# Sliding-window attention: one set of weights for all heads, spread on chip instead of through DRAM

## The chip, the cores and the metric

The kernel runs on one core of a Trainium2 chip. The metric is the device time of one execution in microseconds (us), lower is better. A core has engines with a queue each that work side by side: PE (TensorE, matmuls; PEld is its weight loads), DVE (VectorE), ACT (ScalarE), POOL (GpSimd, used for constants only) and SP (SyncE, which here only issues transfers). PE writes to PSUM, eight banks of 128 partitions by 512 float32; all else is in SBUF, 128 partitions wide. Sixteen DMA engines move data between DRAM and SBUF.

## The reference

A transformer block over 2048 positions of width 512, in bfloat16: an attention with a dilated sliding window (32 heads of 16, each position sees itself and seven earlier ones, two apart), then an MLP with a ReLU gate of width 1376.

```python
def _A_ref(x, wqkv, wo):                       # H = 32, Dh = 16, W = 8, dil = 2
    q, k, v = ...                              # (x @ wqkv), as (3, B, H, S, Dh)
    idx = pos[:, None] - (arange(W) * dil)[None, :]        # masked where < 0
    logits = einsum("bhsd,bhswd->bhsw", q, kg) * Dh ** -0.5
    attn = softmax(where(mask, logits, -1e9))
    o = einsum("bhsw,bhswd->bhsd", attn, vg)
    return o.reshape(B, S, D) @ wo

h  = x + _A_ref(layernorm(x), wqkv, wo)
xn = layernorm(h)
h2 = h + (relu(xn @ W_gate) * (xn @ W_up)) @ W_down
```

## The kernel before

The positions are cut into four chunks of 512 (`CS`). Everything inside a chunk is kept transposed: features on partitions, positions along the row. For each chunk:

1. *Norm and transposes* (`layernorm`): per block of 128 positions DVE takes statistics (L301, L304), ACT makes 1/sqrt (L311, L315), DVE writes the normalised rows `xn` (L324), PE transposes them into PSUM tile `tp` (L330) and ACT evicts that into `xnT` (L333).
2. *QKV* (L362): 12 groups of four matmuls 128x128 by 128x512; ACT evicts each (L370). A row block of 128 features holds 8 whole heads of 16 dims, so there are four row blocks `t`, each with heads of its own.
3. *Scores*: for each row block DVE multiplies q by the eight shifted views of k in one instruction of 128x4096 (L397, tile `big`). PE adds over the 16 dims of a head with column-tiled matmuls of 32 output rows (L409, weights `sel`). Two row blocks make a pair `p`, whose scores fill one PSUM bank: 16 heads by 8 window places.
4. *Softmax* per pair: exponent on ACT (L416), denominator by a matmul with `bmat` (L422), its reciprocal as exp(-ln) on ACT (L425, L428), the product with it on DVE (L431).
5. *Spreading the weights*: the weights (`ex`, 128x512) go to a DRAM tile `scr` (L434), and for each row block 8 transfers (one a head, 128 KB each) read them back, each copied to the 16 partitions of its head (L455), into a tile `big`.
6. *Value sum*: DVE multiplies `big` by the eight shifted views of v (L462), PE adds the eight places with identity matmuls (L466), ACT evicts into `OT` (L470).
7. *Output projection* with `wo` (L486), residual on DVE (L491), norm and transposes as in 1 into `hnT`.
8. *MLP*: 11 blocks of 128 (the last 96) features, up and gate (L508), eviction and ReLU on ACT (L512, L515), product on DVE into `gT` (L518), down-projection (L534), residual on DVE (L538), store by SP (L541).

The order of the work is made by a planner at build time (`Plan.order`): each step has an engine, an assumed duration, its dependencies, the buffers that it takes, and a priority; the engine that can start first takes the step that can start first (of those within 0.02 us, the one of lowest priority number). The result is one fixed order per engine, which the chip follows whatever the true durations are. Priorities put chunk `tk`'s norm at 100·tk - 86, QKV at 100·tk + 10, attention at + 20, its MLP at + 160. Assumed durations are, for instance, 0.216 for a matmul of 512 columns, 0.52 for an ACT eviction, 2.2 for a 128x4096 product.

PSUM before is cut into fixed parts: 3 banks for `mm`, 2 for `od`, 1 for `tp`, 2 for `at`.

Of the kernel before, what the change touches and what calls it, by code (L numbers as in the profile page):

```python
# [8 lines left out]
P = 128  # L9
# [110 lines left out]
def kernel(  # L120
# [11 lines left out]
    nc = tc.nc  # L132
# [17 lines left out]
    HPT = P // DH  # L150
    NPR = NT // 2
# [6 lines left out]
    dr = ctx.enter_context(tc.tile_pool(name="dr", bufs=1, space=bass.MemoryType.DRAM))  # L158
# [30 lines left out]
    scr = [[dr.tile([P, CS], BF16, name=f"scr{c}_{p}") for p in range(NPR)] for c in range(NCK)]  # L189


    for j in range(BPC):
        nc.sync.dma_start(x_sm[:, j:j + 1, :], x_rows[:, j:j + 1, :])
    wq_r = A_wqkv.rearrange("(dt p) f -> p dt f", p=P)
    for c in range(3):
        nc.scalar.dma_start(wqkv_sb[:, :, c * D:(c + 1) * D], wq_r[:, :, c * D:(c + 1) * D])
    for tk in range(1, NCK):
        nc.sync.dma_start(x_sm[:, tk * BPC:(tk + 1) * BPC, :], x_rows[:, tk * BPC:(tk + 1) * BPC, :])
    nc.sync.dma_start(wo_sb[:], A_wo.rearrange("(dt p) f -> p dt f", p=P))
    nc.sync.dma_start(wu_sb[:], B_W_up.rearrange("(dt p) f -> p dt f", p=P))  # L200
    nc.sync.dma_start(wg_sb[:], B_W_gate.rearrange("(dt p) f -> p dt f", p=P))
    nc.sync.dma_start(
# [3 lines left out]


    make_identity(nc, identity[:])
    nc.gpsimd.memset(eps_t[:], EPS)
    nc.gpsimd.memset(sel[:], 0.0)  # L210
    nc.gpsimd.memset(kT[:, :, 0:PADL], 0.0)
    nc.gpsimd.memset(vT[:, :, 0:PADL], 0.0)

    nc.gpsimd.iota(ind_i[:], pattern=[[1, HPT]], base=0, channel_multiplier=0)
    nc.gpsimd.iota(bm_i[:], pattern=[[8, 2], [0, 2], [1, HPT], [0, 4]], base=0, channel_multiplier=0)
    nc.gpsimd.iota(mk_i[:], pattern=[[1, PADL]], base=0, channel_multiplier=0)
    nc.gpsimd.iota(ci[:], pattern=[[0, 4]], base=0, channel_multiplier=1)
    ca = sb.tile([P, 4], I32, name="ca")
    tmp = sb.tile([P, 4], I32, name="tmp")
    V = nc.vector  # L220

    def ts(o, i, s1, op0, s2=None, op1=None):
        if op1 is None:
            V.tensor_scalar(out=o, in0=i, scalar1=s1, scalar2=None, op0=op0)
        else:
            V.tensor_scalar(out=o, in0=i, scalar1=s1, scalar2=s2, op0=op0, op1=op1)

    ts(ca[:, 0:1], ci[:, 0:1], 4, ALU.arith_shift_right)
    ts(tmp[:, 0:1], ci[:, 0:1], 6, ALU.arith_shift_right, 3, ALU.arith_shift_left)
    ts(tmp[:, 1:2], ci[:, 0:1], 2, ALU.arith_shift_right, 7, ALU.bitwise_and)  # L230
    ts(tmp[:, 2:3], ci[:, 0:1], 5, ALU.arith_shift_right, 1, ALU.bitwise_and)
    ts(tmp[:, 3:4], ci[:, 0:1], 3, ALU.bitwise_and)
    V.tensor_copy(out=cf[:, 0:1], in_=ca[:, 0:1])
    tf = sb.tile([P, 4], F32, name="tf")
    V.tensor_copy(out=tf[:], in_=tmp[:])
    V.tensor_tensor(out=cf[:, 1:2], in0=tf[:, 0:1], in1=tf[:, 1:2], op=ALU.add)
    ts(cf[:, 2:3], tf[:, 2:3], 4.0 * DIL, ALU.mult)
    ts(cf[:, 3:4], tf[:, 3:4], 1.0 * DIL, ALU.mult)
    V.tensor_tensor(out=cf[:, 2:3], in0=cf[:, 2:3], in1=cf[:, 3:4], op=ALU.add)
    V.tensor_copy(out=ind_f[:], in_=ind_i[:])  # L240
    V.tensor_copy(out=bm_f[:], in_=bm_i[:])
    V.tensor_copy(out=mk_f[:], in_=mk_i[:])
    ts(ind[:], ind_f[:], cf[:, 0:1], ALU.is_equal)
    ts(bmat[:], bm_f[:], cf[:, 1:2], ALU.is_equal)
    ts(mask[:], mk_f[:], cf[:, 2:3], ALU.is_ge)
    for w in range(4):
        V.tensor_copy(out=sel[:, w, :, w], in_=ind[:])


    xnT_s = slots(2, [P, NT, CS], BF16, "xnT")  # L250
    hnT_s = slots(2, [P, NT, CS], BF16, "hnT")
    qT_s = slots(2, [P, NT, CS], BF16, "qT")
    OT_s = slots(2, [P, NT, CS], BF16, "OT")
    big_s = slots(5, [P, W, CS], BF16, "big")
    gT_s = slots(17, [P, CS], BF16, "gT")
    ex_s = slots(2, [P, CS], BF16, "ex")
# [3 lines left out]
    up_s = slots(3, [P, CS], BF16, "up_sb")  # L260
    gr_s = slots(2, [P, CS], BF16, "gr")
    o_s = slots(3, [P, D], BF16, "o_out")
    st_s = slots(4, [P, V.BN_STATS_DIM], F32, "st")
    mv_s = slots(4, [P, BPC, V.BN_AGGR_DIM], F32, "mv")
    rs_s = slots(4, [P, BPC], F32, "rs")
    mm_s = slots(3, [P, CS], F32, "mm_ps", ps)
    od_s = slots(2, [P, D], F32, "od_ps", ps)
    tp_s = slots(1, [P, NT, P], BF16, "tp_ps", ps)
    at_s = slots(2, [P, CS], F32, "at_ps", ps)

    plan = Plan()
    add = plan.add

# [9 lines left out]
    for tk in range(NCK):  # L283
        xload[tk] = add("LD", 0.0, None, lat=[5.0, 10.5, 12.0, 13.5][tk])
    wload = {"q": add("LD", 0.0, None, lat=7.0), "k": add("LD", 0.0, None, lat=8.0),
             "v": add("LD", 0.0, None, lat=9.0), "o": add("LD", 0.0, None, lat=15.0),
             "u": add("LD", 0.0, None, lat=19.0), "g": add("LD", 0.0, None, lat=23.0),
             "d": add("LD", 0.0, None, lat=27.0)}

    def layernorm(tk, src_dep, dst_slots, pr, groups):  # L290

        dst = Buf(dst_slots)
        mv, rs = Buf(mv_s), Buf(rs_s)
        evs = []
        for grp in groups:
# [21 lines left out]

            l = add("ACT", 0.25, f_ln, ag, pr, take=[rs], use=[mv], lat=AL)
            e = add("ACT", 0.17, f_ex, [l], pr, use=[rs], lat=AL)
            for j in grp:  # L320
                xn, tp = Buf(xn_s), Buf(tp_s)

                def f_xn(j=j, xn=xn):
                    V.tensor_scalar(out=xn.t[:], in0=x_sm[:, tk * BPC + j, :],  # L324
                                    scalar1=mv.t[:, j, 0:1], scalar2=rs.t[:, j:j + 1],
                                    op0=ALU.subtract, op1=ALU.mult)

                def f_tp(xn=xn, tp=tp):
                    for t in range(NT):
                        nc.tensor.transpose(tp.t[:, t, :], xn.t[:, t * P:(t + 1) * P], identity[:])  # L330

                def f_ev(j=j, tp=tp):
                    nc.scalar.copy(out=dst.t[:, :, j * P:(j + 1) * P], in_=tp.t[:])  # L333
# [7 lines left out]
    for tk in range(NCK):  # L341
# [3 lines left out]
        groups = [[0, 1], [2, 3]] if tk == 0 else [[0, 1, 2, 3]]  # L345
        xnT, xev = layernorm(tk, [xload[tk]] * BPC, xnT_s, lnp, groups)
# [4 lines left out]
        if tk == 0:  # L351
            seq = [(c, t) for p in range(NPR) for t in (2 * p, 2 * p + 1) for c in (0, 1)]
            seq += [(2, t) for t in range(NT)]
        else:
            seq = [(c, t) for t in range(NT) for c in (0, 1)] + [(2, t) for t in range(NT)]
        for n, (c, t) in enumerate(seq):
# [3 lines left out]
            def f_mm(c=c, t=t, mm=mm, xnT=xnT):  # L360
                for dt in range(NT):
                    nc.tensor.matmul(mm.t[:], lhsT=wqkv_sb[:, dt, c * D + t * P: c * D + (t + 1) * P],  # L362
                                     rhs=xnT.t[:, dt, :], start=(dt == 0), stop=(dt == NT - 1))
# [18 lines left out]
        OT = Buf(OT_s)  # L382
        oev = {}
        for p in range(NPR):
            prods, pd = [], []
            apr = base + 20 + 6 * p
            for t in (2 * p, 2 * p + 1):
                pb = Buf(big_s)

                def f_pr(t=t, pb=pb, qT=qT, s0=s0):  # L390
                    kb = kT[:, t, PADL + s0: PADL + s0 + CS]
                    k8 = bass.AP(tensor=kb.tensor, offset=kb.offset,
                                 ap=[list(kb.ap[0]), [-DIL, W]] + [list(y) for y in kb.ap[1:]])
                    qb = qT.t[:, t, :]
                    q8 = bass.AP(tensor=qb.tensor, offset=qb.offset,
                                 ap=[list(qb.ap[0]), [0, W]] + [list(y) for y in qb.ap[1:]])
                    V.tensor_tensor(out=pb.t[:], in0=q8, in1=k8, op=ALU.mult)  # L397
# [20 lines left out]
            def f_mk(ex=ex):  # L418
                V.tensor_tensor(out=ex.t[:, 0:PADL], in0=ex.t[:, 0:PADL], in1=mask[:], op=ALU.mult)
# [167 lines left out]
```

## Time and profile before

| | us |
|---|---|
| median of 3 runs (lowest to highest) | 329.92 (328.26 to 330.45) |
| the profiled execution, whole | 326.86 |
| its span, first to last instruction | 325.1 |
| PE busy, in that span | 245.4 |
| DVE busy | 149.0 |
| ACT busy | 123.9 |
| mean clock granted to PE (1 is full) | 0.89 |

The profile is of one execution. A row of the groups of instructions reads: line, engine, operation, output<-inputs, shapes, xcount | busy us in all, mean ns of one | idle time of the engine just before them, and what ended it. A row of the waits reads: who waited <- for whom: us in total, times, longest. The chain that ended last is followed back from the last instruction, each step to what released it. DMA issues show the size of one transfer and the median us from issue to landing. Matmuls are pipelined: the length of a row of several is what counts, not the mean of one.

### The profile page before, as it was taken

To read this page: it belongs to the slowest core of one execution; us is meant where nothing else is said; L and a number is where in the kernel's file an instruction comes from. 1 tells how busy PE (TensorE), PEld (TensorE's weight loads), DVE (VectorE), ACT (ScalarE), POOL (GpSimd) and SP (SyncE) were. 2 spreads that over 40 slices of the span, in tenths; PEclk is the share of its full clock that TensorE was granted. 3 is DMA by queue.
4 is the path that set the end of the run, shared out by engine and by line. 5 is a ranking of instruction groups with operands and counts; after the bars stand their busy time and mean duration, and the time that the engine had idled before them with its cause. 6 is when DMAs were issued, how large, how long until landed. Compare 5 with 4: busy or idle time off the path is not lost.

```text
span 325.1 us, 3266 instructions
## 1 busy us (share of the span) xinstructions
PE 245.4 (75%) x1155; PEld 107.9 (33%) x1176; DVE 149.0 (46%) x235; ACT 123.9 (38%) x227; POOL 1.8 (1%) x14
## 2 busy tenths in 40 slices
PE   0597963489652695974999956999995556989995
PEld 0243421134210242531444422444442122444442
DVE  2989622487222589334131133748423323831222
ACT  2458632045300135732406612317872112226630
POOL 2000000000000000000000000000000000000000
PEclk9999897779856778995999987999998778999999
DMA  8991799939979101990010990010089990010001
GB/s 250 359 381 50 132 127 127 133 49 131 130 117 135 23 0 28 137 112 0 0 50 32 135 124 0 3 48 16 18 135 132 132 132 4 0 49 18 0 16 49
DMA packets 16352, 28.56 MB, mean 88 GB/s; under 512 B 2672, under 2 KB 11216, under 8 KB 16336
## 3 DMA queue, kind: packets, MB, share of 16 engines
q1 hardware_dynamic: 14752, 26.78, 48.6%
q10 hardware_dynamic: 1584, 1.57, 1.5%
q8 instruction: 9, 0.15, 0.2%
q14 instruction: 7, 0.06, 0.1%
HBM read 25.20 MB, written 3.15 MB: 87 GB/s over the span
## 4 chain that ended last, share of the span: by engine, by line
PE 40%; DMA 38%; DVE 8%; SPq 6%; ACT 4%; issue 4%; DVEq 0%; ACTq 0%
DMA big<-scr 33%; PE od_ps L534 12%; PE mm_ps L508 10%; PE mm_ps L362 8%; SPq L455 5%; PE od_ps L466 4%; DVE big L462 4%; DMA scr<-ex 3%; PE od_ps L486 2%; DMA x_sm<-in_A_x_dram 2%; PE at_ps L409 2%; PE tp_ps L330 1%; DVE st L301 1%; ACT xnT L333 1%; ACT rec L428 1%
## 5 line engine op out<-in xcount | busy, mean ns | idle before, releaser
L466 PE MATMUL od_ps<-big,identity 128*128 128x512 bf16 x124 | 45.4, 525 | 49.6 <-DVE big L462 38.5
L462 DVE TENSOR_TENSOR big<-big,vT 128x4096 bf16<-128x4096 bf16 x16 | 36.7, 2292 | 77.2 <-DMA big<-scr 71.8
L508 PE MATMUL mm_ps<-hnT,wu_sb 128*128 128x512 bf16 (+1 forms) x169 | 48.0, 404 | 8.4 <-ACT gr L515 6.4
L362 PE MATMUL mm_ps<-xnT,wqkv_sb 128*128 128x512 bf16 x187 | 47.2, 407 | 1.9 <-ACT xnT L333 1.4
L508 PE MATMUL mm_ps<-hnT,wg_sb 128*128 128x512 bf16 (+1 forms) x174 | 47.6, 395 | 0.4 <-DMA big<-scr 0.2
L466 PEld LDWEIGHTS <-identity 128*128 128x128 bf16 x128 | 14.8, 120 | 75.9 <-issue 37.6
L470 ACT CAST OT<-od_ps 128x512 bf16<-128x512 f32 x16 | 9.4, 585 | 80.4 <-PE od_ps L466 80.4
L534 PE MATMUL od_ps<-wd_sb,gT 128*128 128x512 bf16 (+1 forms) x173 | 39.2, 379 | 0.4 <-DVE x_sm L491 0.3
L518 DVE TENSOR_TENSOR gT<-gr,up_sb 128x512 bf16<-128x512 bf16 (+1 forms) x44 | 18.3, 422 | 45.6 <-ACT gr L515 45.4
L397 DVE TENSOR_TENSOR big<-qT,kT 128x4096 bf16<-128x4096 bf16 x16 | 35.7, 2284 | 4.9 <-ACT kT L370 4.9
L515 ACT ACTIVATE gr<-mm_ps 128x512 bf16<-128x512 f32 (+1 forms) x44 | 26.3, 597 | 29.1 <-PE mm_ps L508 16.3
L512 ACT CAST up_sb<-mm_ps 128x512 bf16<-128x512 f32 (+1 forms) x44 | 25.7, 584 | 14.7 <-PE mm_ps L508 12.3
L362 PEld LDWEIGHTS <-wqkv_sb 128*128 128x128 bf16 x192 | 20.1, 105 | 27.7 <-issue 9.4
L508 PEld LDWEIGHTS <-wu_sb 128*128 128x128 bf16 (+1 forms) x176 | 18.3, 105 | 30.8 <-issue 14.7
L508 PEld LDWEIGHTS <-wg_sb 128*128 128x128 bf16 (+1 forms) x176 | 18.4, 105 | 23.1 <-issue 4.7
L330 PE MATMUL tp_ps<-identity,xn 128*128 128x128 bf16 x128 | 13.6, 235 | 15.1 <-DVE xn L324 9.1
L534 PEld LDWEIGHTS <-gT 128*128 128x128 bf16 (+1 forms) x176 | 17.0, 98 | 20.3 <-issue 0.6
L301 DVE BATCH_NORM_STATS2 st<-x_sm 128x6 f32<-128x512 bf16 x32 | 20.8, 678 | 5.9 <-DMA x_sm<-in_A_x_dram 5.8
L538 DVE TENSOR_TENSOR o_out<-x_sm,od_ps 128x512 bf16<-128x512 bf16 x16 | 11.0, 687 | 24.1 <-PE od_ps L534 24.1
L330 PEld LDWEIGHTS <-xn 128*128 128x128 bf16 x128 | 10.2, 105 | 23.5 <-DVE xn L324 10.0
L486 PE MATMUL od_ps<-wo_sb,OT 128*128 128x512 bf16 x64 | 15.3, 379 | 0.0
L333 ACT COPY hnT<-tp_ps 128x512 bf16<-128x512 bf16 x16 | 9.3, 583 | 15.2 <-PE tp_ps L330 15.2
(49 smaller groups left out, 116.2 us busy)
## 6 DMA issues: line engine op xcount, KB each, us to landing
big<-scr SPq DMA_DIRECT2D x128, 128.0 KB, 7.9
out_dram<-o_out SPq DMA_DIRECT2D x16, 128.0 KB, 1.7
wqkv_sb<-in_A_wqkv_dram ACTq DMA_DIRECT2D x3, 512.0 KB, 5.9
x_sm<-in_A_x_dram SPq DMA_DIRECT2D x3, 512.0 KB, 8.3
wu_sb<-in_B_W_up_dram SPq DMA_DIRECT2D x1, 1376.0 KB, 10.9
wg_sb<-in_B_W_gate_dram SPq DMA_DIRECT2D x1, 1376.0 KB, 13.9
wd_sb<-in_B_W_down_dram SPq DMA_DIRECT2D x1, 1280.0 KB, 15.0
scr<-ex SPq DMA_DIRECT2D x8, 128.0 KB, 1.7
```

The lines of the kernel that those rows point to most:

```text
L301: V.bn_stats(out=st.t[:], in_=x_sm[:, tk * BPC + j, :])
L330: nc.tensor.transpose(tp.t[:, t, :], xn.t[:, t * P:(t + 1) * P], identity[:])
L362: nc.tensor.matmul(mm.t[:], lhsT=wqkv_sb[:, dt, c * D + t * P: c * D + (t + 1) * P], rhs=xnT.t[:, dt, :], start=(dt == 0), stop=(dt == NT ...
L397: V.tensor_tensor(out=pb.t[:], in0=q8, in1=k8, op=ALU.mult)
L462: V.tensor_tensor(out=ab.t[:], in0=ab.t[:], in1=v8, op=ALU.mult)
L466: nc.tensor.matmul(u.t[:], lhsT=identity[:], rhs=ab.t[:, w, :], start=(w == 0), stop=(w == W - 1))
L486: nc.tensor.matmul(od.t[:], lhsT=OT.t[:, t, j * P:(j + 1) * P], rhs=wo_sb[:, t, :], start=(t == 0), stop=(t == NT - 1))
L508: nc.tensor.matmul(mm.t[:fs, :], lhsT=w_sb[:, dt, ft * P: ft * P + fs], rhs=hnT.t[:, dt, :], start=(dt == 0), stop=(dt == NT - 1))
L512: nc.scalar.copy(out=ub.t[:fs, :], in_=um.t[:fs, :])
L515: nc.scalar.activation(out=gr.t[:fs, :], in_=gm.t[:fs, :], func=ACT.Relu)
L518: V.tensor_tensor(out=gt.t[:fs, :], in0=gr.t[:fs, :], in1=ub.t[:fs, :], op=ALU.mult)
L534: nc.tensor.matmul(od.t[:], lhsT=gts[ft].t[:fs, j * P:(j + 1) * P], rhs=wd_sb[:fs, ft, :], start=(ft == 0), stop=(ft == NFT - 1))
```

## The change

It re-cuts the features so that every row block holds dims of all heads. Columns `t, t+4, t+8, ...` of `wqkv` are taken as weights for block `t`, so a row block has 4 dims (`DQ`) of each of the 32 heads (partition = 4·head + dim), and the four blocks add to the same scores. `wo` is loaded with the matching row order. So there is one set of weights per chunk, in two halves `hf` of four window places: `ex` holds 4 places by 32 heads.

- Scores: a product of four places at a time (128x2048, tile `pb`), and per product four column-tiled matmuls with `sel` (128x32), accumulated over the four row blocks.
- Spreading: for each of the eight places one matmul with 32 rows of `ex` and of a matrix `spread` (32 heads to 128 partitions), evicted by ACT into `ab`; all four row blocks use the same `ab`. There is no DRAM tile any more.
- The exponents are not normalised before the value product; the reciprocal `rc` (one per chunk, already in the layout of the output rows) multiplies the finished sum (`f_om`).
- The sum over the eight places stays on PE in chunks 0 and 3 (`PESUM`); in chunks 1 and 2 DVE adds halves in three steps (`f_a`).
- In chunks 1 to 3 the first norm's `xn` is made by ACT (`LNA`), with a small DVE step `nb` ahead of it.
- All PSUM tiles share one pool of eight banks; `xnT`, `hnT`, `qT` and `OT` share nine buffers `quad`. `gT` has 15 buffers instead of 17, `up_sb` and `o_out` 2 instead of 3.
- Loads: x blocks 0 to 3 alternate between SP and ACT, `wqkv` goes behind them on SP, x of chunks 2 and 3 behind `W_gate`. The table load of ACT comes behind its two transfers. Chunk 0's norm runs by single blocks.
- The down-projection of a block of 128 positions is three steps of the plan (7, 3 and 1 matmuls) instead of one of 11.

```diff
-    scr = [[dr.tile([P, CS], BF16, ...) for p in range(NPR)] for c in range(NCK)]
...
-    nc.sync.dma_start(wo_sb[:], A_wo.rearrange("(dt p) f -> p dt f", p=P))
+    nc.sync.dma_start(wo_sb[:], A_wo.rearrange("(p t) f -> p t f", t=NT))
...
+    quad_s = slots(9, [P, NT, CS], BF16, "quad")
+    xnT_s = hnT_s = qT_s = OT_s = quad_s
+    bank_s = slots(8, [P, CS], F32, "bank", ps)
+    mm_s = od_s = tp_s = at_s = bank_s
+    PESUM = (0, 3)
+    LNA = ((0, 1, 1, 1), (0, 0, 0, 0))
...
+                        nc.scalar.activation(out=xn.t[:], in_=x_sm[:, tk * BPC + j, :], func=ACT.Identity,
+                                             bias=nb.t[:, j:j + 1], scale=rs.t[:, j:j + 1])
...
-                    nc.tensor.matmul(mm.t[:], lhsT=wqkv_sb[:, dt, c * D + t * P: c * D + (t + 1) * P],
+                    nc.tensor.matmul(mm.t[:], lhsT=wqkv_sb[:, dt, c * D + t:(c + 1) * D:NT],
...
+        for hf in range(2):
+            for t in range(NT):
+                def f_pr(...):        # q by four shifted views of k, 128 x 2048
+                    V.tensor_tensor(out=pb.t[:], in0=q4, in1=k4, op=ALU.mult)
+                def f_sc(t=t, sc=sc, pb=pb):
+                    for g in range(4):
+                        nc.tensor.matmul(sc.t[g * HB:(g + 1) * HB, :], lhsT=sel[:],
+                                         rhs=pb.t[:, g, :], start=(t == 0), stop=(t == NT - 1),
+                                         tile_position=(0, g * HB))
...
+                def f_bc(g=g, bc=bc, ex=exs[hf]):
+                    nc.tensor.matmul(bc.t[:], lhsT=spread[g * HB:(g + 1) * HB, :],
+                                     rhs=ex.t[g * HB:(g + 1) * HB, :], start=True, stop=True,
+                                     tile_position=(g * HB, 0))
+                def f_be(w=4 * hf + g, bc=bc, ab=ab):
+                    nc.scalar.copy(out=ab.t[:, w, :], in_=bc.t[:])
...
-            b = add("DVE", D2, f_am, [a, b], apr, use=[ex, rc], lat=DL)
-            wr = add("SP", 0.15, f_wr, [b], apr, use=[ex], lat=2.2)
-                rd = add("SP", 0.8, f_rd, [wr], tpr, take=[ab], lat=5.0)
...
+            def f_mu(t=t, ab=ab, mt=mt, s0=s0):
+                V.tensor_tensor(out=mt.t[:], in0=ab.t[:], in1=v8, op=ALU.mult)
+            def f_a(n, mt):
+                V.tensor_tensor(out=mt.t[:, 0:n, :], in0=mt.t[:, 0:n, :], in1=mt.t[:, n:2 * n, :],
+                                op=ALU.add)
+            def f_om(t=t, mt=mt, rc=rc, OT=OT):
+                V.tensor_tensor(out=OT.t[:, t, :], in0=mt.t[:, 0, :], in1=rc.t[:], op=ALU.mult)
+            if tk in PESUM:           # eight identity matmuls into u, then f_om from PSUM
...
-            a = add("PE", 11 * MM, f_dn, gds + [wload["d"]], mb + 5, take=[od], use=gts, lat=PEL)
+            for lo, hi in ((0, 7), (7, 10), (10, NFT)):
+                a = add("PE", (hi - lo) * MM, ..., gds[lo:hi] + [wload["d"], a], mb + 5, take=[od], ...)
```

More of the change, by code (lines that the diff above doesn't have):

```diff
@@ L232 @@
[L232 to L253, printed above, removed]
```

273 lines of the change are left out of this document (134 added, 139 removed).

## Prediction

> **What bounds the kernel now.** I read the page's totals and the chain that ended last, then the waits, then the work by stage.
>
> ```profile
> span 325.1 us, 3266 instructions
> ...
> PE 245.4 (75%) x1155; PEld 107.9 (33%) x1176; DVE 149.0 (46%) x235; ACT 123.9 (38%) x227; POOL 1.8 (1%) x14
> ...
> PE 40%; DMA 38%; DVE 8%; SPq 6%; ACT 4%; issue 4%; DVEq 0%; ACTq 0%
> DMA big<-scr 33%; PE od_ps L534 12%; PE mm_ps L508 10%; PE mm_ps L362 8%; SPq L455 5%; PE od_ps L466 4%; DVE big L462 4%; DMA scr<-ex 3%; PE od_ps L486 2%; DMA x_sm<-in_A_x_dram 2%; PE at_ps L409 2%; PE tp_ps L330 1%; DVE st L301 1%; ACT xnT L333 1%; ACT rec L428 1%
> ...
> big<-scr SPq DMA_DIRECT2D x128, 128.0 KB, 7.9
> ```
>
> PE is busy for 75% of the span, yet the chain that ended last runs through one kind of transfer for a third of it: `big<-scr`, the 128 reads of 128 KB (16.8 MB) that copy each head's attention weights from DRAM to that head's 16 partitions, issued at L455. No engine is full.
>
> ```profile
> DVE big L462 <- DMA big<-scr: 71.8, 15, 8.0
> ```
>
> The wait that ends last is thus the DMA's: the value product L462 stands 71.8 us for it, at most 8.0 at a time, and whatever needs that product stands behind it.
>
> ```profile
> 34.00:69.00 35.00, 22.05 (x101) 9.00 (x103) 16.21 (x9) 11.19 (x20) 0.00 (x0) 0.79 0.96 124
> 69.00:110.00 41.00, 25.34 (x107) 10.04 (x101) 17.11 (x22) 11.35 (x22) 0.00 (x0) 0.79 0.78 109
> 293.00:322.00 29.00, 28.51 (x129) 13.02 (x131) 7.00 (x15) 12.99 (x22) 0.00 (x0) 1.00 0.04 15
> ```
>
> By stage (columns: length, busy us of PE, PEld, DVE, ACT, POOL, then granted clock, DMA share, GB/s): over these 76 us the DMA engines are 96 and 78% busy at only 124 and 109 GB/s, PE is busy for 47 us and its granted clock falls to 0.79. The last MLP (293 to 322) is what PE looks like when nothing holds it: 28.5 us of 29 at clock 1.00.
>
> **The change, part by part.** First PE's costs at full clock, from the chain in order of time (start, length, what) and two rows of other views:
>
> ```profile
> 14.13 9.27 PE mm_ps L362 x33
> 26.86 1.90 PE at_ps L409 x32
> 117.81 1.73 PE od_ps L486 x8
> 119.75 0.98 PE at_ps L409 x16
> 219.38 0.23 PE tp_ps L330 x4
> 321.73 0.69 DVE o_out L538
> ...
> 14.13 12.50 PE L362 MATMUL mm_ps<-xnT,wqkv_sb 128*128 128x512 bf16 x47 [0.67 <-ACT xnT L333]
> 55.23 3.57 PE L466 MATMUL od_ps<-big,identity 128*128 128x512 bf16 x8 [5.18 <-DVE big L462]
> ...
> L422 PE MATMUL at_ps<-ex,bmat 128*128 128x512 bf16 x8 | 3.3, 411 | 0.4 <-DVE ex L419 0.4
> L362 PEld LDWEIGHTS <-wqkv_sb 128*128 128x128 bf16 x192 | 20.1, 105 | 27.7 <-issue 9.4
> ```
>
> A 512-column matmul costs 1.73/8 = 0.216 us. Column-tiled score matmuls cost (1.90 - 0.98)/16 = 0.0575 us each plus about 0.06 per burst. Four transposes cost 0.23.
>
> *Removed outright*: the write of `ex`, the 128 reads and their issue on SP, with all 71.8 us of L462's wait. What is late next is the subject of the rest.
>
> *PE.* Per chunk the weighted sum takes 32 matmuls (L466); afterwards only chunks 0 and 3 (`PESUM`) keep it. Counting 512-column matmuls: 192 (QKV) + 64 (`wo`) + 352 (up, gate) + 176 (down) + 64 (sum) + 8 (denominator) = 856, by 0.216 = 184.9 us. Scores: 128 as before, but in 32 bursts of four, 0.29 each: 9.3 us (7.6 in before's bursts). Spreading, 32 matmuls of 32 rows, not shown by this trace: from 2.3 us (eight bursts of four like the tiled rows) to 13 us (each alone, as L422's lone matmul, 0.41). I take 2.3, since L409 is the nearest row and four become ready together; the upper end stays in the range. Transposes 32 x 0.23 = 7.4. Sum **204 us**; before, the same count gives 920 x 0.216 + 7.6 + 7.4 = 214, against 245.4 busy, so cold clock costs before some 31 us: behind a 5.18 us pause, eight sum matmuls took 3.57 us instead of 1.73.
>
> ```profile
> L462 DVE TENSOR_TENSOR big<-big,vT 128x4096 bf16<-128x4096 bf16 x16 | 36.7, 2292 | 77.2 <-DMA big<-scr 71.8 <-DMA scr<-ex 5.4
> L397 DVE TENSOR_TENSOR big<-qT,kT 128x4096 bf16<-128x4096 bf16 x16 | 35.7, 2284 | 4.9 <-ACT kT L370 4.9
> L301 DVE BATCH_NORM_STATS2 st<-x_sm 128x6 f32<-128x512 bf16 x32 | 20.8, 678 | 5.9 <-DMA x_sm<-in_A_x_dram 5.8
> L518 DVE TENSOR_TENSOR gT<-gr,up_sb 128x512 bf16<-128x512 bf16 (+1 forms) x44 | 18.3, 422 | 45.6 <-ACT gr L515 45.4
> L324 DVE TENSOR_SCALAR xn<-x_sm,mv,rs 128x512 bf16<-128x512 bf16 x32 | 12.1, 406 | 5.2 <-PE tp_ps L330 4.6 <-ACT rs L315 0.6
> L538 DVE TENSOR_TENSOR o_out<-x_sm,od_ps 128x512 bf16<-128x512 bf16 x16 | 11.0, 687 | 24.1 <-PE od_ps L534 24.1
> L491 DVE TENSOR_TENSOR x_sm<-x_sm,od_ps 128x512 bf16<-128x512 bf16 x16 | 10.7, 680 | 2.5 <-PE od_ps L486 2.5
> L304 DVE BATCH_NORM_AGGREGATE mv<-st 128x2 f32<-128x6 f32 x32 | 4.6, 169 | 0.0
> L431 DVE TENSOR_TENSOR ex<-ex,rec 128x512 bf16<-128x512 bf16 x8 | 3.3, 417 | 8.0 <-ACT rec L428 8.0
> ```
>
> *DVE*, from 149.0 us. A bf16 product costs 0.417 us at 512 elements and 2.292 at 4096, so 0.523 ns per element between: 1.22 us at 2048 and 0.69 at 1024. The key products become 32 of 2048: 39.0 for 35.7 (+3.3). The normalising product L431 goes (-3.3). 12 of 32 `xn` go to ACT (-4.5), three small `nb` come (+0.5). Chunks 1 and 2 add by halves: 8 x (1.22 + 0.69 + 0.42) = +18.6. Division at the end: 8 from SBUF at 0.42 and 8 from PSUM at 0.68 (as L491) = +8.8. Constants change by under 1. Sum **172 us**.
>
> ```profile
> L470 ACT CAST OT<-od_ps 128x512 bf16<-128x512 f32 x16 | 9.4, 585 | 80.4 <-PE od_ps L466 80.4
> L428 ACT ACTIVATE rec<-lnd 128x512 bf16<-128x512 f32 x8 | 5.1, 642 | 0.1
> L425 ACT ACTIVATE lnd<-at_ps 128x512 f32<-128x512 f32 x8 | 4.8, 606 | 0.5 <-PE at_ps L422 0.5
> L311 ACT ACTIVATE rs<-mv,eps_t 128x4 f32<-128x4 f32 (+1 forms) x9 | 2.7, 303 | 9.6 <-DVE mv L304 9.6
> L315 ACT ACTIVATE rs<-rs 128x4 f32<-128x4 f32 (+1 forms) x9 | 1.9, 210 | 0.2
> ```
>
> *ACT*, from 123.9 us. Gone: 16 `OT` copies (-9.4) and half of L425 and L428 (-5.0). Added: 32 evictions of spread weights, 0.585 each as L470 (+18.7), eight per chunk, and the value product waits for the last of them: a new wait, behind which stand on DVE, in fixed order, the three other value products and whatever key products or `gT` were placed later, and behind those PE's down-projection; 12 `xn` with two operands read per partition, bounded by L428's 0.64 and that plus twice the 0.093 by which L311 (bias per partition) exceeds L315: I take 0.8 (+9.6; 0.6 would be 7). Two more small pairs (+1.0). Sum **139 us**.
>
> ```profile
> GB/s 250 359 381 50 132 127 127 133 49 131 130 117 135 23 0 28 137 112 0 0 50 32 135 124 0 3 48 16 18 135 132 132 132 4 0 49 18 0 16 49
> ...
> 11.61 0.60 PE tp_ps L330 x4
> 12.87 0.60 PE tp_ps L330 x4
> ...
> 18.35 8.89 DVE L397 TENSOR_TENSOR big<-qT,kT 128x4096 bf16<-128x4096 bf16 x4 [1.42 <-ACT kT L370]
> 127.58 0.58 PE L508 MATMUL mm_ps<-hnT,wu_sb 128*128 128x512 bf16 x1 [0.91 <-ACT hnT L333]
> ...
> 120.73 0.98 PE od_ps L486 x4
> ...
> 110.00:125.00 15.00, 12.13 (x64) 5.27 (x66) 13.40 (x16) 5.48 (x10) 0.00 (x0) 0.77 0.01 1
> ```
>
> *Start.* QKV began at 14.13. The three later transposes of chunk 0 began 1.26 apart (one `tp` slot, each behind the last eviction), with setup products of DVE between; eight shared banks let them follow the 0.59 us evictions, some 2 us less. With `wqkv` behind x on SP instead of beside it, x lands earlier and the weights later, which I price at a gain of 1, bounds 3 and -2. Start about 11.
>
> *Weights in steps of four* (L362's `lhsT`): 192 loads. Before, each took 0.105 us beside a 0.216 us matmul, so twice that is hidden; I take nothing, and price the rest as a rival. `wo` in 4 KB rows, x of chunks 2 and 3 behind `wg`, and the down-projection in three pieces: nothing, since the loads run at over 350 GB/s in the second and third slice and MLP 0 cannot begin before about 59 us (next). Without that cover a late x would cost its wait. Fewer buffers (15 `gT`, 2 `up_sb`, 2 `o_out`, two `mt`, one set of eight PSUM banks): nothing, as long as the matmuls that free a buffer and those that need it run on the same PE one after the other; if not, a blocked matmul holds up all behind it. On SP the 16 stores now stand behind no reads.
>
> *First attention.* Before, chunk 0's products began at 18.35, right behind the first key eviction; now about 15.3. Eight products 9.8 and chunk 1's statistics 4 x 0.8: 28.3. Scores 0.3, exponent 0.6, mask 0.15, spreading with four evictions 2.4, hops 0.5: 32.2; ACT also evicts chunk 1's QKV then, so 35. Value products 4 x 2.29 and divisions 4 x 0.68: 47. Last sum 1.73 and division 0.68: 49. From the first `wo` matmul (117.6) to the first MLP matmul (127.6) before took 10 us, so MLP 0 at **59**. PE has 54 us of work ready for these 48 (QKV 0 to 2, scores, sum, `wo`); but ACT has about as much (36 + 16 + 16 evictions by 0.585 = 40, `xn` 6, exponents and logarithms 8), DVE too. I let PE do 40 of 48.
>
> *After that.* PE has 204 - 40 - 28.5 = 136 us before MLP 3; DVE, from MLP 0 to MLP 3, has about 45 + 45 + 36 for the three chunks (gate 4.6, output 2.8, products 9.8, values 9.2, adds 9.3 except in chunk 3, divisions 2, residual and norm 7.4), less 10 of products done ahead: 116, and three exposed chains of about 5. PE ends last, narrowly: 59 + 136 = 195, plus MLP 3 at 28.5 and 3.4 from the last residual's start to the end (321.73 to 325.1): 227. Holes where PE and DVE hand over, with cold matmuls behind them: I allow 4. Span **231**.
>
> Check from below: start 11 + 204 - 1 (chunk 0's transposes lie before it) + 2.3 for the cold first QKV (12.5 for 47, instead of 10.2) + 3.4 = 220 if PE never idles.
>
> The profiled execution took 326.86 for a span of 325.1 (+1.8), and lies 0.9% under the median of 329.92. 231 + 1.8 = 232.8 by the profile's measure; I forecast **233**, leaving the 0.9% to the range.
>
> A rule that speaks against the change: the Trainium skill, TensorEngine Tiling (Array Packing), section Key Properties, says that changing the tiling mode drains the array. The 0.06 us per burst agrees with a small drain. By that rule with a drain as long as a lone matmul's excess the sum would be the third rival's.
>
> **The rivals.**
>
> 1. *DVE's chains are the bound* (0.20). For it: DVE's work rises while PE's falls, the order is fixed ahead with assumed durations (0.52 us for an eviction that takes 0.585), and every chunk has one serial chain through four engines. Against: before's dense stretch 110 to 125 has DVE 13.4 of 15 us busy with the same operations. Price: DVE must do 172 - 7.4 = 165 us before MLP 3; at 75% density that is 7 (before DVE's work begins in earnest) + 220 = 227, plus 31.9 for MLP 3 and the end: 259; at 80%, 245. With the launch **242 to 262**. The Trainium skill, TensorE: Matmul & The Clock Gate, Part 1, puts half clock behind about 3.4 us of idle; the 3.57 us row agrees, so each such hole would cost more than its length.
>
> 2. *PE never starves* (0.14): the sum's floor, 217 to 225 with the launch. Against: ACT's and DVE's full first 59 us.
>
> 3. *Each tiled burst drains the array* (0.05). L422's 0.41 is 0.19 over a streaming matmul. Score bursts (32) and spread matmuls (32, each alone) at 0.19: 12 us, so **245**. Against: before's burst ended and `wo` went on without a gap (119.75 + 0.98 = 120.73).
>
> 4. *Strided weight loads stall QKV* (0.03 for 260 or more, of it 0.02 for slower than before). At the 192 loads of L362, it decides once a load exceeds 0.216 us. At 0.43 it costs 41 us: 274. To end slower than 327 it takes (327 - 233)/192 + 0.216 = 0.71 us a load, nearly seven times the present. Against: nothing here shows it; for it only that the trace has no strided load. The change not doing what it says (transfers remaining) is excluded by the diff: no DRAM tile is left.
>
> **How the numbers follow.** The forecast itself (226 to 241) has 0.58. The range 221 to 252 takes in the bounds of start, spreading and `xn` (-3, +11, +-2), most of rival 2, rival 3 and half of rival 1; about 0.17 lies outside. About 1% is what a measurement of this kernel can tell from no change. Faster 0.97, within 1% 0.01, slower 0.02.
>
> **What would show it.** DMA share near zero after some 28 us; DVE 172, ACT 139, PE busy 205 to 220 at a mean clock above 0.93; score bursts about 0.29 us; spread matmuls in fours; MLP 0 at 55 to 63 and MLP 3 at 192 to 204; QKV groups of four still 0.86. I would be wrong if PE stands for `mt` or `ab` in the middle chunks for over 15 us in all, if weight loads of L362's successor show over 0.2 us, or if ACT's spread evictions arrive long after their turn.

## The result, and the profile after

| | before | after |
|---|---|---|
| median of the runs (us) | 329.1 | 230.7 (230.5 to 232.6) |
| after to before, 95% interval | | 0.703 (0.697 to 0.710) |
| profiled execution, and its span | 326.9, 325.1 | 230.6, 228.5 |
| PE busy, and idle in the span | 245.4, 79.7 | 212.4, 16.1 |
| DVE busy, ACT busy | 149.0, 123.9 | 164.6, 129.9 |
| mean granted clock of PE | 0.89 | 1.00 |

The forecast was 233 (221 to 252). One profile further down, that of the kernel before with the spread on PE, is of an execution slower than the others of its kernel (306.3 against a median of 301.1 us), so its busy times are somewhat high.

From the page of the changed kernel, totals and the chain that ended last:

```profile
PE 212.4 (93%) x1144; PEld 98.3 (43%) x1144; DVE 164.6 (72%) x263; ACT 129.9 (57%) x251; POOL 1.6 (1%) x13
...
PE 85%; DVE 8%; ACT 4%; DMA 1%; issue 1%; DVEq 0%
PE bank L516 34%; PE bank L353 18%; PE bank L542 17%; PE bank L494 6%; DVE mt L456 4%; PE bank L472 4%; PE bank L392 3%; ACT quad L324 2%; DVE pb L388 2%; PE bank L321 2%; PE bank L420 1%; DMA x_sm<-in_A_x_dram 1%; ACT ab L425 1%; DVE st L283 1%; PE bank L433 1%
```

DMA held 38% of the chain before and now 1%; PE went from 40 to 85%. By stage (columns as before: length, busy us of PE, PEld, DVE, ACT, POOL, granted clock, DMA share, GB/s), cut at the first QKV matmul and at the first matmul of MLP 0 and of MLP 3:

```profile
0.00:10.50 10.50, 2.07 (x16) 1.58 (x17) 5.45 (x22) 4.89 (x13) 1.65 (x13) 1.00 0.81 257
10.50:67.00 56.50, 54.37 (x321) 25.25 (x321) 47.04 (x71) 40.92 (x82) 0.00 (x0) 1.00 0.29 102
67.00:196.60 129.60, 127.40 (x677) 58.63 (x676) 103.98 (x154) 71.19 (x135) 0.00 (x0) 1.00 0.04 12
196.60:225.20 28.60, 28.55 (x133) 12.87 (x130) 7.42 (x16) 12.93 (x22) 0.00 (x0) 1.00 0.06 19
```

Of PE's 16.1 us of idle time 8.4 lie before the first QKV, 3.3 behind the last matmul, and only 4.4 in the 215 us between. The span is PE's work and its two ends.

PE's work itself is more than the count of matmuls gives. From the chain in order of time:

```profile
10.55 12.08 PE bank L353 x48
28.87 0.33 PE bank L392 x4
29.20 0.99 PE bank L353 x4
50.36 0.55 PE bank L392 x8
66.95 18.99 PE bank L516 x88
112.83 0.54 PE bank L433 x2
```

The columns are start, length, and the group. A burst of four column-tiled score matmuls, which run side by side, takes 0.33 us where one untiled matmul takes 0.216 (18.99/88), and the four untiled matmuls behind it take 0.99 instead of 0.86. So a burst costs 0.22 to 0.24 us beyond its streaming, half of it booked on the work behind it (0.33 - 0.22, and 0.99 - 0.86). The two untiled denominator matmuls right behind a spread burst show the same: 0.54 instead of 0.43. Two bursts that run together take 0.55, which is twice the streaming and one price of 0.11: the price goes with each change of tiling, into the burst and out of it, and not with the matmuls.

### The profile page after: what moved, and what is told of

Its sections match the earlier page's. It is cut to its first block, busy times and chain, and to the rows that moved or that the text cites. A ratio compares the mean times of both kernels' runs of the same rounds, so it can differ in the third digit from the quotient of the medians.

```text
span 228.5 us, 3028 instructions
## 1 busy us (share of the span) xinstructions
PE 212.4 (93%) x1144; PEld 98.3 (43%) x1144; DVE 164.6 (72%) x263; ACT 129.9 (57%) x251; POOL 1.6 (1%) x13
## 4 chain that ended last, share of the span: by engine, by line
PE 85%; DVE 8%; ACT 4%; DMA 1%; issue 1%; DVEq 0%
PE bank L516 34%; PE bank L353 18%; PE bank L542 17%; PE bank L494 6%; DVE mt L456 4%; PE bank L472 4%; PE bank L392 3%; ACT quad L324 2%; DVE pb L388 2%; PE bank L321 2%; PE bank L420 1%; DMA x_sm<-in_A_x_dram 1%; ACT ab L425 1%; DVE st L283 1%; PE bank L433 1%
## 5 line engine op out<-in xcount | busy, mean ns | idle before, releaser
L353 PE MATMUL bank<-quad,wqkv_sb 128*128 128x512 bf16 x192 | 46.2, 390 | 0.7 <-ACT quad L324 0.7
L516 PE MATMUL bank<-quad,wu_sb 128*128 128x512 bf16 (+1 forms) x176 | 45.2, 379 | 0.3 <-ACT quad L324 0.3
L516 PE MATMUL bank<-quad,wg_sb 128*128 128x512 bf16 (+1 forms) x176 | 45.2, 379 | 0.0
L456 DVE TENSOR_TENSOR mt<-ab,vT 128x4096 bf16<-128x4096 bf16 x16 | 36.5, 2285 | 4.6 <-ACT ab L425 4.5
L542 PE MATMUL bank<-wd_sb,gT 128*128 128x512 bf16 (+1 forms) x176 | 39.2, 379 | 0.0
L388 DVE TENSOR_TENSOR pb<-quad,kT 128x2048 bf16<-128x2048 bf16 x32 | 38.0, 1215 | 1.4 <-PE bank L392 1.3
L523 ACT ACTIVATE gr<-bank 128x512 bf16<-128x512 f32 (+1 forms) x44 | 26.5, 603 | 17.1 <-PE bank L516 16.9
L520 ACT CAST up_sb<-bank 128x512 bf16<-128x512 f32 (+1 forms) x44 | 26.0, 590 | 16.2 <-PE bank L516 15.5
L546 DVE TENSOR_TENSOR o_out<-x_sm,bank 128x512 bf16<-128x512 bf16 x16 | 10.9, 683 | 12.3 <-PE bank L542 12.2
L324 ACT COPY quad<-bank 128x512 bf16<-128x512 bf16 x32 | 17.0, 598 | 4.5 <-PE bank L321 4.4
L459 DVE TENSOR_TENSOR mt<-mt 128x2048 bf16<-128x2048 bf16 (+2 forms) x24 | 18.3, 772 | 0.1
L425 ACT CAST ab<-bank 128x512 bf16<-128x512 f32 x32 | 16.9, 612 | 0.6 <-PE bank L420 0.4
```

Source lines behind the costliest of these rows:

```text
L353: nc.tensor.matmul(mm.t[:], lhsT=wqkv_sb[:, dt, c * D + t:(c + 1) * D:NT], rhs=xnT.t[:, dt, :], start=(dt == 0), stop=(dt == NT - 1))
L388: V.tensor_tensor(out=pb.t[:], in0=q4, in1=k4, op=ALU.mult)
L425: nc.scalar.copy(out=ab.t[:, w, :], in_=bc.t[:])
L456: V.tensor_tensor(out=mt.t[:], in0=ab.t[:], in1=v8, op=ALU.mult)
L459: V.tensor_tensor(out=mt.t[:, 0:n, :], in0=mt.t[:, 0:n, :], in1=mt.t[:, n:2 * n, :], op=ALU.add)
L516: nc.tensor.matmul(mm.t[:fs, :], lhsT=w_sb[:, dt, ft * P: ft * P + fs], rhs=hnT.t[:, dt, :], start=(dt == 0), stop=(dt == NT - 1))
```

## The experiments

Each row is the median of the runs, its ratio to the kernel before with the 95% interval, and what PE did in the profiled execution.

| run | us | ratio | PE busy, idle |
|---|---|---|---|
| changed kernel | 230.7 | 0.703 (0.697 to 0.710) | 212.4, 16.1 |
| one set, through DRAM | 234.0 | 0.711 (0.708 to 0.715) | 210.9, 22.3 |
| one set, through DRAM, reads in the old form | 243.6 | 0.741 (0.736 to 0.746) | 215.8, 26.4 |
| before, with the spread on PE | 301.1 | 0.915 (0.911 to 0.920) | 277.5, 27.0 |
| re-cut and spread alone, side edits undone | 258.5 | 0.788 (0.783 to 0.793) | 234.7, 22.6 |
| all sums on PE | 243.0 | 0.739 (0.736 to 0.742) | 225.2, 16.2 |
| all sums on DVE | 246.8 | 0.751 (0.748 to 0.754) | 205.1, 40.8 |
| fixed PSUM banks | 247.6 | 0.754 (0.751 to 0.758) | 223.7, 21.7 |
| score bursts of eight | 231.0 | 0.706 (0.702 to 0.710) | 210.3, 19.4 |
| clock opened early | 231.5 | 0.707 (0.704 to 0.711) | 216.6, 13.0 |
| clock early, x of chunk 2 later | 231.8 | 0.709 (0.706 to 0.713) | 215.1, 15.1 |
| these two and bursts of eight | 228.0 | 0.695 (0.690 to 0.700) | 213.1, 13.2 |
| x later and bursts of eight | 228.0 | 0.694 (0.691 to 0.697) | 210.3, 15.2 |

My theory behind the first four: cutting the rows so that one set of weights serves all heads is what counts, and PE is then the bound. The rivals: that the on-chip spread is the gain, and that DVE's chain sets the end.

**One set, but through DRAM.** In the changed kernel `ex` is written to DRAM again and read back in place of the eight spread matmuls and evictions.

```diff
-    nc.tensor.matmul(bc.t[:], lhsT=spread[...], rhs=ex.t[...], tile_position=(g * HB, 0))   # x8
-    nc.scalar.copy(out=ab.t[:, w, :], in_=bc.t[:])                                          # x8
+    nc.sync.dma_start(d[:], ex.t[:])                                    # x2
+    nc.sync.dma_start(ab.t[c:P:DQ, 4 * hf:4 * hf + 4, :], src)          # x8, 128 KB each
```

> The changed kernel (230.7), but its one set of weights per chunk goes through DRAM again: two writes of 128 KB, then eight reads of 128 KB a chunk (1 MB) instead of 32 reads (4 MB). Theory A, cutting the rows so that one set serves all heads is what counts, and PE is the bound now: the shorter transfers hide behind PE work, ACT loses 32 evictions, PE loses 32 spread matmuls (some 6 us with the mode changes): 224 to 236. Rival, the transfer's latency is what counted: each chunk's chain gets some 8 us longer than the on-chip path and PE starves: 245 or more.

234.0, inside the theory's range. DMA issues and, from the chain by engine, DMA's share:

```profile
ab<-scr SPq DMA_DIRECT2D x32, 128.0 KB, 2.6
...
PE 82%; ACT 7%; DVE 7%; issue 2%; DMA 1%
```

Reads of the same 128 KB land after 2.6 us instead of 7.9. Replacing DRAM by PE and ACT is worth some 3 us of the 98, and as the two intervals overlap not even that is sure; the rest, side edits included, is there with the weights still going through DRAM. But these reads go to every fourth partition, the old ones to 16 neighbours, so the next run took the old form.

**One set, reads in the old form.** The same number of bytes, but `ab` then holds weights of other heads and places, so this kernel computes something else.

```diff
-    nc.sync.dma_start(ab.t[c:P:DQ, 4 * hf:4 * hf + 4, :], src)          # x8
+    src = bass.AP(..., ap=[[0, DH], [32 * CS, 2], [1, 4 * CS]])         # x8, behind both writes
+    nc.sync.dma_start(ab.t[h * DH:(h + 1) * DH, :, :].rearrange(...), src)
```

> As the run with one set through DRAM, but its eight reads a chunk have exactly the form of the kernel before: 128 KB each, into 16 neighbouring partitions, in rows of 4 KB, behind both writes (so the weights in the tile are those of other heads and places; the output is not the reference's). In the kernel before such reads landed after 7.9 us, in the one-set run after 2.6. Theory A1, the number of sets counts (eight reads instead of 32 a chunk): 232 to 242, reads landing after 5 to 8 us and hidden. Rival, the form of the reads counts (16 neighbouring partitions are slow to write): 250 or more.

243.6, just above the theory's range and below the rival's. The issues, and the chain by engine and by line:

```profile
ab<-scr SPq DMA_DIRECT2D x32, 128.0 KB, 5.1
...
PE 53%; DVE 18%; DMA 14%; SPq 5%; ACT 4%; issue 4%; DVEq 0%; ACTq 0%
PE bank L355 13%; PE bank L545 13%; PE bank L519 11%; DMA ab<-scr 10%; DVE mt L459 7%; PE bank L475 6%; PE bank L497 6%; DVE mt L462 5%; SPq L428 5%; DMA scr<-ex 3%; ACT quad L326 3%; PE bank L394 2%; DVE gT L529 2%; DVE pb L390 1%; DMA x_sm<-in_A_x_dram 1%
```

In this form (which also waits for both halves) the reads land after 5.1 us and DMA is on the chain again with 14%, for a price of 10 us. So a quarter of the old reads, in the old form, still leaves 84 of the 98 us, side edits included; the form matters too, but as the smaller part. What in the form counts, the neighbouring partitions, the longer rows, eight reads at once or the wait for both halves, this run does not separate.

**Before, with the spread on PE.** Rows still hold whole heads; each row block's eight places are spread by matmuls of 32 rows and evicted.

```diff
-    wr = add("SP", 0.15, f_wr, [b], apr, use=[ex], lat=2.2)
-    rd = add("SP", 0.8, f_rd, [wr], tpr, take=[ab], lat=5.0)
+    nc.tensor.matmul(bc.t[:], lhsT=spread[r:r + 32, w4, :], rhs=ex.t[r:r + 32, :], tile_position=(r, 0))
+    nc.scalar.copy(out=ab.t[:, w, :], in_=bc.t[:])                      # x8 for each row block
```

(`ex` has four buffers and `gT` 16.)

> The kernel before, whose row blocks still hold whole heads, with only the spreading changed: 128 matmuls of 32 rows and 128 evictions by ACT instead of 128 reads through DRAM. Theory A: the wait for DMA goes, but the same weights are now spread four times over: ACT 124 + 128 x 0.6 = 200 us, PE's floor 214 + 128 spread matmuls at 0.08 to 0.2 = 225 to 240, and a chunk's path is longer: 255 to 285, so that the on-chip spread alone gives about two thirds of the gain. Rival, the spread alone is the whole gain: 235 or less. Rival, ACT's queue eats it: 300 or more.

301.1: worse than I thought, 28 us of the gain and not 45 to 75, and just inside the rival by which ACT's queue eats it. The totals and the two groups of the spread:

```profile
PE 277.5 (91%) x1280; PEld 108.7 (36%) x1304; DVE 150.9 (50%) x244; ACT 186.5 (61%) x355; POOL 2.0 (1%) x15
...
L462 ACT CAST big<-at_ps 128x512 bf16<-128x512 f32 x128 | 71.5, 593 | 26.2 <-PE at_ps L458 25.8
L458 PE MATMUL at_ps<-ex,spread 32*128 32x512 bf16 x128 | 45.5, 414 | 3.8 <-ACT big L462 2.1 <-DVE ex L437 0.8
```

Four sets need 128 evictions, 71.5 us of ACT, in place of 32, but ACT is not what holds the kernel: it is busy for 61% of the span, and PE stands for its evictions for only 2.1 us. PE is busy for 91%. The 128 spread matmuls are 45.5 us of PE, against 3.9 for the 32 of the changed kernel: almost all go alone or in twos between untiled work, and four in a row use the same 32 rows, so that two of them take 0.53 us, one behind the other, where four of the changed kernel take 0.33. How much of this comes from having four sets, and how much from the two PSUM banks and the shared rows, no run separates. The on-chip spread alone is not the gain.

**The sum over the places, all on PE or all on DVE.**

```diff
-    PESUM = (0, 3)
+    PESUM = (0, 1, 2, 3)        # the first run
+    PESUM = ()                  # the second
```

> The changed kernel with the sum over the eight places on PE in all four chunks: PE 64 matmuls more (13.8 us), DVE some 16 us less. Theory A, PE never starves and its work sets the end: 242 to 247. Rival, DVE's chain sets the end: 226 or less. No change would mean that the two are balanced.

243.0, as the theory has it. The totals:

```profile
PE 225.2 (93%) x1186; PEld 104.3 (43%) x1208; DVE 151.3 (63%) x239; ACT 130.9 (54%) x251; POOL 1.6 (1%) x13
```

The 64 matmuls more are 13.8 us; 12.8 us more busy time on PE came out as 12.3 us more time, with the idle time unchanged (16.2). DVE's relief, from 164.6 to 151.3, brought nothing.

> The changed kernel with all sums on DVE: PE 13.8 us less, DVE some 16 us more (172 to 181 by its rows). Theory A, PE's work sets the end wherever DVE keeps up: 217 to 224, less than the whole 13.8 since chunk 0's and chunk 3's sums stand ahead of an MLP. Rival, DVE sets the end: 240 or more.

246.8: here the rival holds. PE is busy for 7.3 us less (64 matmuls fewer would be 13.8, but the mean granted clock is 0.94) and stands 24.7 us more. The totals:

```profile
PE 205.1 (83%) x1060; PEld 93.8 (38%) x1080; DVE 179.8 (73%) x287; ACT 129.4 (53%) x251; POOL 1.6 (1%) x13
```

and the largest of its groups of waits (sum, times, longest):

```profile
PE bank L494 <- DVE quad L463: 16.6, 4, 8.2
```

PE waits 16.6 us at the output projection for DVE's division. So PE is the bound of the changed kernel, with DVE close behind in chunks 0 and 3, where nothing else lies between the attention and an MLP.

**Re-cut and spread alone.** The side edits undone: sums on PE, all `xn` on DVE, fixed banks and buffers, one-piece down-projection, loads and start as before (`gT`, `up_sb` and `o_out` keep their fewer buffers).

```diff
-    PESUM = (0, 3)
+    PESUM = (0, 1, 2, 3)
+    LNA = ((0, 0, 0, 0), (0, 0, 0, 0))
+    mm_s, od_s, tp_s, at_s = slots(3, ...), slots(2, ...), slots(1, ...), slots(2, ...)
```

> The changed kernel with its re-cut rows and on-chip spread, but every side edit undone: all sums on PE, all xn on DVE, fixed PSUM banks 3/2/1/2, fixed pairs of buffers for xnT, hnT, qT and OT, the down-projection in one piece, the loads and the start as before. Theory A, PE's work is the bound: 231 + 12 for the sums (as the run with all sums on PE, 243), + 3 for the start, + 2 to 8 for waits on banks: 246 to 256. Rival, the side edits carry much of the gain: 270 or more.

258.5, between the two, nearer to the theory (246 to 256) than to the rival (270 or more).

```profile
PE 234.7 (91%) x1208; PEld 105.7 (41%) x1208; DVE 155.4 (60%) x248; ACT 126.2 (49%) x235; POOL 1.7 (1%) x13
```

So 70 of the 98 us are the re-cut with its spread, 28 the side edits; of these 28, 22 are PE's busy time (234.7 against 212.4). How the 70 divide between the re-cut and the spread when the side edits are missing, no run shows.

**Fixed PSUM banks** (3, 2, 1 and 2) in the changed kernel:

```diff
-    bank_s = slots(8, [P, CS], F32, "bank", ps)
-    mm_s = od_s = tp_s = at_s = bank_s
+    mm_s, od_s, tp_s, at_s = slots(3, ...), slots(2, ...), slots(1, ...), slots(2, ...)
```

> The changed kernel with PSUM cut in fixed parts of 3, 2, 1 and 2 banks as before, for matmul groups, output sums, transposes and attention. Eight spread matmuls a chunk then share two banks with the scores, and their evictions gate them. If the banks hide waits: 233 to 238; if PE's order is dense anyway: 230 to 232.

247.6: neither. I expected waits of at most 7 us; it is 16.9, and 11.3 of them are PE's busy time (223.7 against 212.4). The spread matmuls as a group (busy time, mean ns of one), in the changed kernel:

```profile
L420 PE MATMUL bank<-ex,spread 32*128 32x512 bf16 x32 | 3.9, 384 | 0.0
```

With fixed banks:

```profile
L422 PE MATMUL at<-ex,spread 32*128 32x512 bf16 x32 | 10.6, 390 | 0.1
```

One of them there in the chain, with the group behind it:

```profile
31.65 0.32 PE at L422
31.97 0.99 PE mm L355 x4
```

With two banks the four matmuls of a half don't go together. In PE's order of time 22 go alone and ten in twos, mostly between untiled groups: 27 stretches of some 0.32 us instead of ten, with 0.99 for the four matmuls behind. The 17 stretches more (3.7 us of streaming) and 32 changes of tiling more (96 instead of 64, 0.11 each: 3.5 us) are 7 of the 11.3 us; much of the rest is a lower clock (the first QKV takes 13.0 us instead of 12.1, and the mean granted clock is 0.985). Sharing eight banks is what makes the spread cheap: it lets the four matmuls of a half go together.

**Price of a burst.** Score matmuls of two row blocks together:

```diff
+    if t % 2:      # one PE step for the matmuls of two products
+        scd.append(add("PE", 0.6, both f_sc, ..., take=[sc], use=[both pb], lat=PEL))
-    pb_s = slots(2, ...); gT_s = slots(15, ...)
+    pb_s = slots(3, ...); gT_s = slots(14, ...)
```

> The changed kernel with score matmuls in 16 bursts of eight (two row blocks together) instead of 32 of four; three product buffers instead of two and 14 gT instead of 15 make room. In the changed kernel a burst of four takes 0.33 us and the matmul group behind it 0.98 instead of 0.86. If each burst pays a fixed price for changing the tiling (0.10 + 0.12): 16 bursts less save 3.5 us of PE, the time is 226.5 to 228.5. If the price goes with the matmuls, or DVE's products now wait for buffers: 230 to 233.

231.0, the rival's range: PE's busy time fell by 2.1 us, the time did not. The score matmuls as a group in the changed kernel:

```profile
L392 PE MATMUL bank<-pb,sel 128*32 128x512 bf16 x128 | 12.0, 388 | 3.3 <-DVE pb L388 3.3
```

and in bursts of eight:

```profile
L392 PE MATMUL bank<-pb,sel 128*32 128x512 bf16 x128 | 10.0, 385 | 0.2
```

The score matmuls take 10.0 instead of 12.0 us, so the fixed price is real. I had expected 3.5 us, for 16 bursts less; but bursts that follow one another without untiled work between them share a change of tiling. Counted in PE's order of time the changed kernel has 64 changes and this one 44, and 20 times 0.11 is 2.2 us.

The planner's new order left PE 3.3 us more idle, most of it just ahead of MLP 0 (PE in order of time):

```profile
70.67 0.40 PE L321 MATMUL bank<-identity,xn 128*128 128x128 bf16 x4 [1.99 <-DVE xn L315]
72.02 1.15 PE L519 MATMUL bank<-quad,wu_sb 128*128 128x512 bf16 x3 [0.96 <-ACT quad L324]
72.96 1.92 PE L519 MATMUL bank<-quad,wg_sb 128*128 128x512 bf16 x4
74.67 1.79 PE L519 MATMUL bank<-quad,wu_sb 128*128 128x512 bf16 x4
76.30 1.03 PE L519 MATMUL bank<-quad,wg_sb 128*128 128x512 bf16 x4
```

It stands 1.99 and 0.96 us for the norm of chunk 0, starts MLP 0 at 72.0 instead of 66.9, and there two groups of four take 1.7 us each instead of 0.86.

**The start.** 60 matmuls of 128 columns ahead of the first transposes, into a bank not yet in use:

```diff
+    for _ in range(60):
+        nc.tensor.matmul(wb.t[:, 0:P], lhsT=identity[:], rhs=identity[:], start=True, stop=True)
```

> The changed kernel with 60 matmuls of 128 columns by the identity put ahead of the first transposes on PE, into a bank that is not yet used; they end before the first xn is ready. QKV of chunk 0 took 12.1 us for 48 matmuls, 10.3 at full speed. If the clock is opened by earlier work: QKV 0 starts at 10.5 as before or 0.3 sooner and takes 10.4 us, the time is 228.4 to 229.5. If the first matmuls wait on something else (weights still landing, ACT): no change, 230.5.

231.5: no gain, though the mechanism works. PE in order of time (first QKV, then the first score burst that waits; in brackets the idle time ahead):

```profile
10.26 10.53 PE L358 MATMUL bank<-quad,wqkv_sb 128*128 128x512 bf16 x48 [0.74 <-ACT quad L329]
24.98 0.40 PE L397 MATMUL bank<-pb,sel 128*32 128x512 bf16 x4 [2.98 <-DVE pb L393]
```

DVE's statistics of chunk 2 in the chain:

```profile
21.72 1.29 DVE st L288 x2
```

The stage behind the wait:

```profile
26.00:28.00 2.00, 1.88 (x8) 0.55 (x7) 2.00 (x3) 0.54 (x1) 0.00 (x0) 0.50 0.05 18
```

QKV 0 takes 10.5 us instead of 12.1 and ends 2 us sooner. Then PE stands 3.0 us for key products, because DVE's order puts the statistics of chunk 2 ahead of them, and these wait for x until 21.7; by 26 the clock is down to half. In the changed kernel DVE stands there too, 4.5 us at the longest:

```profile
DVE st L283 <- DMA x_sm<-in_A_x_dram: 10.7, 3, 4.5
```

So the next three runs moved those statistics behind the products, by a later assumed load:

```diff
-        xload[tk] = add("LD", 0.0, None, lat=[4.5, 11.0, 22.0, 24.0][tk])
+        xload[tk] = add("LD", 0.0, None, lat=[4.5, 11.0, 27.0, 29.0][tk])
```

> The changed kernel with two edits at the start: the 60 small matmuls that open the clock early (QKV of chunk 0 ended 2 us sooner with them, but PE then stood 3 us for key products), and 27 instead of 22 us assumed by the planner for the load of x of chunk 2, so that DVE's statistics of chunk 2 stand behind chunk 0's key products; in the changed kernel DVE stood 4.5 us at those statistics for x. If that stand is what ate the early clock: 226 to 228.5. If PE's later order takes it back: 230 to 231.5.

> The two edits at the start and the score bursts of eight together. If each frees PE time and PE is the bound, the gains add: 222.5 to 225.5. If they meet in the same holes: 226 to 229.

> The kernel of the run with all three edits (228.0) without the 60 matmuls that open the clock: later load assumed for x of chunk 2, score bursts of eight. If the early clock has a part in the gain: 229.5 to 231. If the other two make it together: 227 to 228.5.

The early clock with the later statistics gives 231.8, just above the second case and no gain; MLP 0 begins at 66.9 as in the changed kernel. With the bursts of eight it is 228.0, with the early clock or without: the second case of both expectations, so the early clock has no part in the gain. PE's busy time is that of the bursts run, its idle time 4.2 us less:

```profile
PE 210.3 (93%) x1144; PEld 97.7 (43%) x1144; DVE 164.4 (73%) x263; ACT 130.2 (58%) x251; POOL 1.6 (1%) x13
```

In the run without the early clock PE does not stand ahead of MLP 0 for more than 0.2 us and begins it at 67.8, so the bursts' gain is kept. Why the later statistics with the early clock bring nothing was not followed further. 228.0 is the best version here; its interval (0.691 to 0.697) just touches the changed kernel's (0.697 to 0.710), and the two were not timed side by side, so about 1% faster is the most that can be said.

## Why the prediction was right

**The bound and its removal**: as forecast. What comes next was PE, by the narrow margin over DVE that the sum gave; the two `PESUM` runs show both sides of it.

**Durations of new operations.** From the groups of the changed kernel:

```profile
L388 DVE TENSOR_TENSOR pb<-quad,kT 128x2048 bf16<-128x2048 bf16 x32 | 38.0, 1215 | 1.4 <-PE bank L392 1.3
L476 DVE TENSOR_TENSOR quad<-bank,rec 128x512 bf16<-128x512 f32 x8 | 5.5, 682 | 1.3 <-PE bank L472 1.3
L425 ACT CAST ab<-bank 128x512 bf16<-128x512 f32 x32 | 16.9, 612 | 0.6 <-PE bank L420 0.4
L312 ACT ACTIVATE xn<-x_sm,nb,rs 128x512 bf16<-128x512 bf16 x12 | 9.5, 819 | 0.3 <-DVE nb L301 0.3
L353 PEld LDWEIGHTS <-wqkv_sb 128*128 128x128 bf16 x192 | 21.2, 116 | 21.8 <-issue 5.5
```

Key products 1.215 us (I took 1.22), division from PSUM 0.682 (0.68), spread evictions 0.612 apart from overlap, 16.9 in all (I took 18.7), `xn` on ACT 0.819 (0.8). Weight loads in steps of four: 116 ns instead of 105, hidden; rival 4 fell.

**DVE 172 and ACT 139** were 164.6 and 129.9. The groups were right, the total was not: neighbouring records overlap, so groups added to a total overcount (DVE's eleven largest groups sum to 174).

**PE 204** was 212.4: the term of the tiled bursts was mis-sized. I allowed 0.06 us a burst, 2.4 for 32 score and eight spread bursts; each change of tiling costs about 0.11, and 64 of them are 7.0. The first QKV's cold clock is 1.7 more (12.08 instead of 10.37) and the first 16 transposes 1.1 (2.07 instead of 0.92). These are 7.4 of the 8.4 us; the last 1 us is not traced. The price is rival 3's, to which I gave 0.05; its 245 did not come, since the spread matmuls mostly go in fours and PE stands less than I allowed. I argued against it with a row that I misread: before's chain went on at 119.75 + 0.98 = 120.73 without a gap, but the next line, 0.98 for four matmuls that stream in 0.86, had the price in it. The Trainium skill, TensorEngine Tiling (Array Packing), Key Properties, has this drain; the trace agrees, and gives the size that the page does not.

**First attention.** I had the last sum and its division done by 49; the last sum ended at 49.5. But MLP 0 began at 66.9, not 59, because PE was not waiting: it did QKV of chunk 2 in between. I let PE do 40 of 48 us; it did 54.4 of 56.5. The error in place cancelled: MLP 0 came later, less was left behind it (127.4 instead of 136, with 2.2 of holes for my 4), and MLP 3 began at 196.6 for the forecast 195.

In sum the bound and what comes next were right, but that the time came out within 1% is in part luck: I took PE's work 8 us too short (204, it was 212.4) and its idle time 11 us too long (231 - 204 = 27, it was 16.1). What held was rivals 2 and 3 at once: PE never starves, and each burst costs. Rival 1 fell: PE stands for DVE's value products for 0.6 us in all.

## What to carry to other kernels

When a copy through DRAM is the bound, ask first how many copies the data layout needs: one set instead of four, with the side edits, brought 84 to 95 of the 98 us while the copy still went through DRAM. Once PE is dense, every PE microsecond counts one for one, so move work to the engine that has room only until that engine's own chain shows (here two chunks of four), and keep small tiled matmuls together, which here took enough free PSUM banks. Read the length of the step behind a burst, not only the gap.

## What the runs showed of the hardware

A change of tiling has no gap in the records: four score matmuls that stream in 0.216 us take 0.33, and the group behind takes 0.11 to 0.13 more. A single spread matmul between untiled work costs 0.32 and 0.13. Four spread matmuls in different rows take 0.33 together (changed kernel); two in the same 32 rows take 0.53 (before, with the spread on PE).

The granted clock is not shown at the start. In the changed kernel the stage from 12 to 13 us reads 1.00 with three matmuls in it, where the one from 15 to 16 us has seven:

```profile
12.00:13.00 1.00, 1.00 (x3) 0.30 (x2) 1.00 (x2) 0.55 (x1) 0.00 (x0) 1.00 1.04 411
15.00:16.00 1.00, 1.00 (x7) 0.48 (x6) 1.00 (x3) 0.96 (x4) 0.00 (x0) 1.00 1.03 407
```

The weight loads in order of time:

```profile
11.36 0.15 PEld L353 LDWEIGHTS <-wqkv_sb 128*128 128x128 bf16 x1 [0.28 <-issue]
11.78 0.15 PEld L353 LDWEIGHTS <-wqkv_sb 128*128 128x128 bf16 x1 [0.28 <-issue]
```

They begin 0.42 us apart, twice the 0.216 of a matmul at full clock. The clock was halved again behind 3.0 us of idle time (0.50 from 26 to 28 us in the run with the early clock), and in the run with bursts of eight behind 1.99 and 0.96 us with four transposes between them (1.7 us for four matmuls).

Reads of 128 KB from DRAM landed after 2.6 us in rows of 1 KB to every fourth partition (four issued together, from one source), and after 5.1 us in rows of 4 KB where each copies one source to 16 neighbours (eight together).
